# New orders for all five engines behind the prologue of a fused attention and feed-forward kernel

## The chip, the core and the metric

The kernel runs on one core of a Trainium2 chip. The core has a matrix engine (TensorE, in the profile PE, with weight loads as PEld), VectorE (DVE), ScalarE (ACT), GpSimd (POOL) and SyncE (SP). Each engine works through its own list of instructions strictly in order, and engines wait for each other by semaphores. Matrix results land in PSUM, which has eight banks; 16 DMA engines carry data, from queues that SP and POOL fill (ACT issues one store at the end).

The metric is the device time of one launch in microseconds, as the median of a few runs without a profiler.

## The reference

Attention over 4 batches, 8 heads, 768 positions and 64 channels, with a sliding window of 128 positions and 4 sink positions; its output, 3072 tokens of 512 channels, goes through an RMS norm and a gated feed-forward layer (FFN) of width 1536:

```python
scores = scale * np.matmul(q, k.transpose(0, 1, 3, 2))
keep = is_sink | in_window
a = softmax(np.where(keep, scores, -1e9))
x = (a @ v), heads side by side          # 3072 x 512
xn = x / np.sqrt(np.mean(x * x, -1) + 1e-6) * rms_g
g = xn @ w_gate
return (g * sigmoid(g) * (xn @ w_val)) @ w_out
```

Inputs and output are float32.

## The kernel before

The tokens are cut into 24 blocks of 128 (six per batch). Each block goes through the same stages.

- *Loads.* POOL issues DMAs that load q, k and v of a block and change them to bf16 on the way (`load_bf16` L360, `load_v` L364), and the weights `wg`, `wv`, `wo` (L406, L412).
- *Transposes.* q and k are needed with channels on the partitions. Blocks 0 to 5 are transposed on TensorE (`pe_t` L452) and copied out of PSUM by ACT or DVE (`copy_t` L459). From block 6 on, SP issues a DMA transpose (`dma_t` L466).
- *Scores.* TensorE computes them for keys of the block and queries of this block and the next (`scores` L492, `scores_last` L508, `tri_scores` L570). They need k of the block and q of this and the next block. ACT takes exponentials (L519, L543, L579), DVE masks them (L527, L554, L591), from block 16 on POOL does (L533, L604).
- *Attention times v.* `av` (L613 to L628), in two halves per block. DVE divides by the row sums (`normal` L667, L668), ACT takes the sum of squares (`square` L677), POOL a root (`root` L684), DVE scales the block (`spread` L711, tile `xr`). The result is transposed, for blocks 0 to 5 on TensorE (`pe_x` L726, copied at L732), then by a DMA that SP issues (`dma_x` L738), into tile `xnt`.
- *FFN.* Four blocks make a group G, 0 to 5. Gate and value products are made in chunks of one PSUM bank (`mms` L995, tiles `g` and `v`): in group 0 four times 128 columns of weights by one block of tokens (16 matmuls), in groups 1 and 2 two weight chunks by two blocks (8 matmuls), then one chunk by four blocks (4 matmuls). ACT takes a tanh of the gate (L1002, tile `th`), DVE makes the product `p` (L1008), which frees the gate's bank, and `hT` (L1018), which frees the value's bank. `project` (L1028, tile `o`) runs in three quarters of four matmuls per block, ACT evacuates (`evacuate` L1036, tile `osb`, four buffers) and SP stores (L1040).

The order of everything is written out by hand in tables ahead of the function. The function first lists 1093 numbered steps, each with what it needs and gives; a step is one call of a small function on one engine. `ORDER` holds one list of step numbers per engine, `TURNS` says from which engine's list the next step is taken when the program is written down, and `BANKS` says which PSUM bank each step that takes one gets:

```python
for c in "".join(turns.split()):
    e, ops = ids[c]
    o = self.ops[next(ops)]
    assert o["needs"] <= given, o["gives"]
    for s in o["takes"]:
        i = self.held[s] = int(next(banks))
        assert i not in owner, s
        owner[i] = s
    for s in o["drops"]:
        assert owner.pop(self.held[s]) == s
```

So the tables decide what each engine does after what; the waits follow from the data, the banks and the buffers. The step numbers that the prediction speaks of:

| step | engine | what it is |
|---|---|---|
| 245, 300, 387, 422, 542 | PE | scores of blocks 3, 6, 11, 13, 20 |
| 252, 254 | PE | attention times v, block 3, its two halves |
| 261, 263, 280, 282 | PE | transposes of q4, k4, q5, k5 |
| 262, 264, 281, 283 | ACT or DVE | copies of these out of PSUM |
| 250, 251 | DVE | masks of block 3 |
| 253, 255, 256, 257, 258 | DVE, DVE, ACT, POOL, DVE | two normalisations, square, root 3, scaling of block 3 |
| 259, 260, 297 | PE, ACT or DVE | transposes of x3 and their copy; the copy for block 5 |
| 647, 648, 649, 650 | PE, PE, ACT, DVE | group 0, weight chunks 4 to 7, third block of tokens: gate, value `u(0,4,256)`, tanh, product |
| 639, 640 | ACT, DVE | tanh and product of chunks 8 to 11, second block |
| 692, 697 | PE | the first two gate chunks of group 1 |
| 852, 853 | PE | gate and value chunk (3,0) of group 3 |
| 858, 863, 882 | PE | value chunks (3,1) and (3,2), gate chunk (3,6) |
| 58, 59, 64, 65, 61 | POOL | loads of q6, k6, q7, k7, q8 |
| 74, 80, 312, 334, 350 | POOL | loads of k11 and k13; roots 6, 7, 8 |
| 386, 401, 421 | SP | DMA transposes of k11, k12, k13 |
| 681, 756 | SP | stores of group 0, block 1, and group 1, block 0 |

Of the kernel before, what the change touches and what calls it, by code (L numbers as in the profile page):

```python
# [76 lines left out]
692 693 300 698 712 679 323 309 702 307 687-689 331 329 703 707 717 339 317 713 718 355  # L77
# [14 lines left out]
218 227 229 228 230 196 614 221 237 619 240 629 634 644 649 624 262 639 246 248 247 281  # L92
249 283 266-269 256 198 285 287 654 260 659 664 275 669 293 297 675 699 685 694 301 303
304 302 714 324-327 704 311 690 333 680 709 719 340 318 341-343 356-359 349 320 372 755
373-375 734 365 388 724 390 381 749 729 739 744 760 405 403 404 784 406 779 423 424 396
425 426 774 789 799 794 413 432 765 419 439 809 440 441 770 442 455 814 456 824 457 458
448 804 471-474 835 464 829 819 489 491 504-507 524 525 840 526 483 527 497 854 859 869
514 864 850 879 874 894 884 536 520 543-546 899 889 909 845 562 904 563-565 581 555
582-584 934 944 949 574 600 602 959 939 593 964 954 969 915 974 925 920 608 984 979 930
989 1024 1019 1010 1014 1029 1044 1039 1005 1054 1034 1049 1000 1069 1064 1059 995 1085  # L100
1075 1080 1088 1089
# [23 lines left out]
""",  # L125
    "SP": """
# [18 lines left out]
"""  # L145
BANKS = """
0123456701234567012345645645635654353153753470347203563513613256506154632712712475602405
4062430145376241536207134527063456237056514705145415743610547601345716403571263425076134
2510677432510645612036514027635014726145732153570650471621506423710614725634726531027465
4614062576120357230575467145620741546205741632573401567234015321764537465127546246315270  # L150
1215273072504102313672065312675316
# [1009 lines left out]
```

## Time and profile before

| | |
|---|---|
| median of 3 runs | 239.07 us (238.98 to 239.96) |
| the profiled execution's own time | 241.29 us |
| its span, first to last instruction | 239.6 us |
| TensorE busy | 230.0 us (96%) |
| DVE, ACT, POOL busy | 165.8, 118.3, 103.5 us |
| granted TensorE clock | 1.000 |
| DMA, POOL's queue (q0) | 81,760 packets, 84.3% of 16 engines' span |
| DMA, SP's queue (q1) | 35,074 packets, 31.8% |
| load of q, k, v, issue to landing, median | 6.2, 6.9, 6.5 us |
| DMA transpose of q, k, of x | 4.7, 4.8, 2.5 us |

A line of the timeline has start and length in us, engine, source line, operation, what it writes and reads, how many were merged, and in brackets the engine's idle time before it with what ended that. A line of waits has engine and line, whom it waited for, the total in us, how often, and the longest. The chain follows the work that ended last back through what released it. An `SPq` line is SP issuing a DMA. TensorE's matmuls are pipelined: the length of a line is not its cost, the distance to the next start is.

### The profile page before, as it was taken

What the parts mean: (1) busy time and instruction counts of PE and PEld (TensorE: products, weight loads), DVE (VectorE), ACT (ScalarE), POOL (GpSimd) and SP (SyncE); (2) the same over time, 40 slices, a digit from 0 to 9 for tenths busy, and PEclk for the clock granted to TensorE, in tenths of its full rate; (3) what the DMA queues carried; (4) which work ended last, traced back from release to release, by engine and by line L of the source; (5) the groups of instructions that cost most, each with busy time, mean ns of one, the idle gap of its engine ahead of it and who ended that gap; (6) DMA issues with size and microseconds to landing.
All of it is one profiled execution on the core that took longest, in us unless ns stands there. A gap on an engine that the chain in (4) does not pass through costs nothing.

```text
span 239.6 us, 5770 instructions
## 1 busy us (share of the span) xinstructions
PE 230.0 (96%) x2306; PEld 146.5 (61%) x2330; DVE 165.8 (69%) x356; ACT 118.3 (49%) x260; POOL 103.5 (43%) x137
## 2 busy tenths in 40 slices
PE   7988999999999997999999999999999999999994
PEld 5667997967685785866786544454444444444443
DVE  2599888866997898887976689784775246537520
ACT  4676559418686455636574651755531421233112
POOL 7975894059275376219297580438410000000000
PEclk9999999999999999999999999999999999999999
DMA  9999999999999999989999999303500210401024
GB/s 123 147 183 193 185 175 193 155 94 158 162 128 148 158 159 144 130 162 167 132 127 155 180 173 175 79 13 31 81 0 0 47 39 27 172 3 48 0 88 175
DMA packets 117004, 28.20 MB, mean 118 GB/s; under 512 B 107121, under 2 KB 114033, under 8 KB 116978
## 3 DMA queue, kind: packets, MB, share of 16 engines
q0 software_dynamic: 81760, 13.90, 84.3%
q1 hardware_dynamic: 35074, 13.74, 31.8%
q8 instruction: 18, 0.29, 0.5%
q10 hardware_dynamic: 144, 0.20, 0.2%
q14 instruction: 8, 0.07, 0.1%
HBM read 28.35 MB, written 6.29 MB: 145 GB/s over the span
## 4 chain that ended last, share of the span: by engine, by line
PE 84%; DMA 7%; POOL 5%; issue 1%; SPq 1%; ACT 0%; DVE 0%; POOLq 0%; ACTq 0%
PE o L1028 25%; PE g L995 24%; PE v L995 24%; DMA wg<-in_moe_w_gate_dram 4%; DMA qkT<-k 3%; PE s L570 3%; PE av L628 2%; PE av L623 2%; POOL v L364 1%; PE o_last L1048 1%; POOL k L360 1%; POOL wg L406 1%; POOL q L360 1%; PE s L492 1%; POOL wv L406 1%
## 5 line engine op out<-in xcount | busy, mean ns | idle before, releaser
L995 PE MATMUL v<-xnt,wv 128*128 128x128 bf16 (+2 forms) x524 | 71.4, 281 | 0.4 <-DMA wv<-in_moe_w_val_dram 0.2
L995 PE MATMUL g<-xnt,wg 128*128 128x128 bf16 (+2 forms) x525 | 71.1, 282 | 0.6 <-DMA wg<-in_moe_w_gate_dram 0.4
L1002 ACT ACTIVATE th<-g 128x512 bf16<-128x512 f32 x72 | 41.4, 600 | 51.0 <-PE g L995 49.8
L1028 PE MATMUL o<-wo,hT 128*128 128x512 bf16 x259 | 65.4, 379 | 1.1 <-issue 0.2
L1008 DVE SCALAR_TENSOR_TENSOR p<-th,g 128x512 bf16<-128x512 bf16 x72 | 48.2, 681 | 23.2 <-ACT th L1002 22.8
L1018 DVE TENSOR_TENSOR hT<-p,v 128x512 bf16<-128x512 bf16 x72 | 48.2, 685 | 13.7 <-PE v L995 9.8
L995 PEld LDWEIGHTS <-wv 128*128 128x128 bf16 x528 | 43.2, 98 | 19.7 <-DMA wv<-in_moe_w_val_dram 0.6
L995 PEld LDWEIGHTS <-wg 128*128 128x128 bf16 x528 | 42.7, 98 | 20.2 <-issue 0.9
L684 POOL TENSOR_TENSOR rp<-ms,nhalf 128x1 f32<-128x1 f32 x21 | 13.4, 637 | 69.2 <-ACT sq L677 69.2
L1028 PEld LDWEIGHTS <-hT 128*128 128x128 bf16 x276 | 25.9, 98 | 27.7 <-issue 0.2
L579 ACT ACTIVATE e<-s 128x384 bf16<-128x384 f32 x52 | 22.5, 500 | 8.0 <-PE s L570 8.0
L677 ACT ACTIVATE sq<-xall 128x516 bf16<-128x516 bf16 (+1 forms) x24 | 15.2, 634 | 16.6 <-DVE xall L668 16.6
L1036 ACT ACTIVATE osb<-o 128x512 f32<-128x512 f32 x23 | 13.6, 600 | 18.9 <-PE o L1028 15.6
L364 POOL DMA_DIRECT2D v<-in_v_dram x24 | 21.8, 911 | 0.6 <-DMA wv<-in_moe_w_val_dram 0.4
L711 DVE SCALAR_TENSOR_TENSOR xr<-xall,rp,gb 128x512 bf16<-128x512 bf16 x21 | 16.6, 789 | 7.4 <-POOL rp L684 7.4
L668 DVE TENSOR_TENSOR xall<-av,rden 128x256 bf16<-128x256 f32 x48 | 20.4, 424 | 1.7
L360 POOL DMA_DIRECT2D q<-in_q_dram x23 | 20.9, 915 | 0.9 <-POOLq L1142 0.8
L360 POOL DMA_DIRECT2D k<-in_k_dram x23 | 20.8, 909 | 0.9 <-DMA wv<-in_moe_w_val_dram 0.4
L543 ACT ACTIVATE e<-s 128x512 bf16<-128x512 f32 (+1 forms) x36 | 15.3, 516 | 3.6 <-PE s L492 2.5
L604 POOL TENSOR_SCALAR_AFFINE_SELECT e<-e 128x512 bf16<-128x512 bf16 x20 | 13.5, 693 | 6.7 <-ACT e L579 6.5
L628 PE MATMUL av<-v,e 128*128 128x65 bf16 x192 | 16.2, 193 | 0.0
L667 DVE RECIPROCAL rden<-av 128x4 f32<-128x4 f32 x48 | 8.4, 176 | 11.2 <-PE av L628 10.9
(82 smaller groups left out, 180.1 us busy)
## 6 DMA issues: line engine op xcount, KB each, us to landing
out_dram<-osb SPq DMA_DIRECT2D x23, 256.0 KB, 3.6
v<-in_v_dram POOLq DMA_DIRECT2D x24, 128.0 KB, 6.5
q<-in_q_dram POOLq DMA_DIRECT2D x23, 128.0 KB, 6.2
k<-in_k_dram POOLq DMA_DIRECT2D x23, 128.0 KB, 6.9
wo<-in_moe_w_out_dram POOLq DMA_DIRECT2D x2, 768.0 KB, 9.7
wg<-in_moe_w_gate_dram POOLq DMA_DIRECT2D x5, 256.0 KB, 9.1
wv<-in_moe_w_val_dram POOLq DMA_DIRECT2D x5, 256.0 KB, 8.0
qkT<-q SPq DMA_TRANSPOSE x18, 4.7
```

The lines of the kernel that those rows point to most:

```text
L360: nc.gpsimd.dma_start(out=T[name, g], in_=block_of(src, g))
L364: nc.gpsimd.dma_start(out=V16[b][:, t, :, 0:D], in_=block_of(v, g))
L543: nc.scalar.activation(out=e_tile(g)[:, x:x + 2, n0 * P:n1 * P], in_=ps.rearrange("p (j c) -> p j c", c=256)[:, :, n0 * P:n1 * P], func=AC ...
L579: nc.scalar.activation(out=e_tile(g)[:, x:x + 2, 0:TW], in_=BANK.pop(("s", g, u, hi))[:, 0:2 * TW].rearrange("p (j c) -> p j c", c=TW), fu ...
L628: nc.tensor.matmul(out=dest, lhsT=T["e", g][:, x, 0:P], rhs=V16[b][:, t, h, :], start=(t == 0), stop=True, skip_group_check=True,)
L668: nc.vector.tensor_tensor(out=T["x16", g][:, 4 * u:4 * u + 4, :], in0=pvv[:, :, 0:D], in1=rden.unsqueeze(2).to_broadcast((P, 4, D)), op=AL ...
L711: nc.vector.scalar_tensor_tensor(out=T["xr", g], in0=xall[:, g % 3, 0:DM], scalar=r, in1=gb, op0=ALU.mult, op1=ALU.mult,)
L995: nc.tensor.matmul(out=ps[:, i * n:(i + 1) * n], lhsT=w_sb[:, kt, ft * P:(ft + 1) * P], rhs=T["xnt", G][:, kt, cols], start=(kt == 0), sto ...
L1002: nc.scalar.activation(out=T["th", key], in_=BANK[("g", key)], func=ACT.Tanh, scale=0.5,)
L1008: nc.vector.scalar_tensor_tensor(out=T["p1", key], in0=T.pop(("th", key)), scalar=1.0, in1=BANK.pop(("g", key)), op0=ALU.add, op1=ALU.mult,)
L1018: nc.vector.tensor_tensor(out=T[hk][:, i:i + n, cols], in0=T.pop(("p1", key)).rearrange("p (n c) -> p n c", n=n), in1=BANK.pop(("v", key)) ...
L1028: nc.tensor.matmul(out=BANK[("o", G, tb)], lhsT=T["h", G, ft // 4][:, ft % 4, tb * P:(tb + 1) * P], rhs=wo[:, ft, :], start=(ft == 0), sto ...
```

## The change

The tables were made anew, with DMA transposes and stores counted at the times that the last trace shows. The source of the steps is the same, so no instruction is added, removed or changed in shape. All five lists differ from a point behind the prologue on (at about 25 us in the profile of before), and so do `TURNS` and `BANKS`. Four steps change engine: the PSUM copies 260, 281, 283 and 297 go from ACT to DVE. Everything else stays on its engine at another place.

```diff
--- before.py
+++ after.py
@@ -72,83 +72,83 @@
 136 170 150 113 199 124 175 180 168 166 187 137 142 149 201 135 126 130 185 165 122 162
 121 132 203 129 140 222 147 204 209 241 145 163 224 214 191 216 156 138 116 195 114 226
 612 146 148 160 133 151 613 167 161 243 220 233 127 235 159 131 627 117 617 632 628 239
-618 647 642 633 643 622 637 623 261 638 245 648 263 280 652 282 265 197 252 254 653 284
-677 672 271 273 259 682 657 658 662 667 668 289 291 663 278 673 683 684 678 296 674 697
-692 693 300 698 712 679 323 309 702 307 687-689 331 329 703 707 717 339 317 713 718 355
-708 752 345 347 753 371 319 754 757 758 363 361 732 722 733 759 387 379 737 377 747 723
-727 738 728 742 748 743 402 782 392 394 777 778 422 797 772 787 773 783 411 788 762 409
-767 768 430 792 428 763 793 764 769 438 807 798 808 822 454 812 446 802 444 813 832 833
-470 834 462 460 817 827 803 823 818 837 838 503 839 479 481 828 493 847 495 848 523 849
-862 867 510 512 852 853 857 877 842 534 858 843 863 868 532 872 878 892 873 844 882 542
-897 893 883 887 907 902 888 561 551 908 903 553 898 580 932 942 947 917 933 948 572 570
...
+618 642 633 647 643 622 637 623 261 638 245 263 280 652 282 265 254 252 653 197 284 682
+677 259 648 657 662 672 271 273 658 667 668 289 291 663 683 673 678 278 674 296 684 692
+693 697 300 698 712 679 702 323 687 309 307 688 689 703 713 331 329 707 708 717 339 317
+718 752-754 319 355 347 345 757 758 371 722 723 361 363 759 732 737 733 727 747 387 379
+377 728 748 742 738 767 743 768 402 394 782 777 772 392 797 783 422 773 792 409 778 411
+762 787 763 428 788 793 430 798 769 764 438 807 812 808 822 813 454 446 444 802 837 838
+803 832 470 833 462 460 827 817 823 839 828 818 834 479 481 847 848 842 843 503 849 862
+857 852 844 872 495 858 493 863 877 867 523 853 878 873 512 892 510 887 868 902 532 534
+893 882 883 888 542 907 927 903 897 908 928 561 553 898 917 551 918 580 919 929 570 572
...
 """,
     "ACT": """
 25 21 23 200 178 176 179 177 183 181 182 184 169 189 223 205-207 212 208 213 210 192 211
-218 227 229 228 230 196 614 221 237 619 240 629 634 644 649 624 262 639 246 248 247 281
-249 283 266-269 256 198 285 287 654 260 659 664 275 669 293 297 675 699 685 694 301 303
...
-373-375 734 365 388 724 390 381 749 729 739 744 760 405 403 404 784 406 779 423 424 396
...
+218 227 229 228 230 196 614 221 237 619 629 240 644 634 624 262 649 639 248 246 249 247
+266-268 256 198 654 269 285 287 659 664 669 275 293 675 694 685 699 303 301 714 302 304
...
     "DVE": """
 0 2 8 1 3 6 12 11 15 7 173 171 14 13 188 4 186 194 202 190 193 242 225 215 217 316 219
-231 232 234 236 615 238 620 616 630 621 244 635 631 5 636 645 646 625 626 650 640 641
-651 264 250 251 253 255 270 258 288 655 656 286 272 274 660 661 665 277 290 666 292 295
-279 670 700 671 695 696 701 306 315 305 715 310 308 328 705 332 330 313 706 335 710 720
...
+231 232 234 236 615 238 616 620 630 631 645 621 646 635 625 244 636 626 650 264 640 281
+251 250 283 255 253 641 258 260 270 651 655 286 665 656 660 288 274 661 272 418 290 292
+277 295 279 670 297 666 671 695 700 701 696 315 305 306 715 705 310 308 328 706 716 332
...
     "POOL": """
 26 9 10 27-29 32 35 31 33 38 36 30 39 34 40 42 43 41 44 46 48 45 49 47 50 51 54 55 37 53
-52 56 57 59 64 58 65 257 61 276 60 294 66 68 67 62 70 71 73 63 312 74 334 69 72 79 77 83
-76 350 80 82 75 366 382 92 78 97 89 85 91 81 88 84 397 86 414 94 433 100 87 95 107 109
-90 98 449 93 475 103 478 465 477 96 476 490 492 110 99 106 101 484 528 531 529 498 530
...
+52 56 57 257 64 59 58 60 65 61 276 294 73 71 66 68 67 62 63 70 312 79 334 69 76 77 83 74
+82 72 350 80 366 75 382 78 84 85 81 88 91 86 97 397 89 414 433 87 93 90 94 92 95 98 449
+100 465 475 478 476 477 109 99 104 107 96 102 103 105 101 106 484 490 492 110 498 531
...
 """,
     "SP": """
-20 22 24 17 16 19 18 321 299 298 322 337 353 338 369 354 370 385 676 314 336 386 401 681
-420 352 400 368 756 436 421 437 452 384 686 487 468 399 521 691 453 761 469 416 488 501
-502 540 435 522 451 467 559 771 597 598 836 486 766 578 541 579 851 841 560 517 500 539
...
+20 22 24 17 16 19 18 298 299 322 321 337 354 353 338 385 676 369 370 314 336 386 681 420
+401 400 352 368 436 421 437 468 452 487 384 399 761 756 691 453 686 469 416 521 501 435
+488 502 766 451 467 522 771 540 559 846 541 597 578 579 486 851 500 836 560 598 517 539
...
 TURNS = """
 ASDDDDSPGPPDDPPPSPPPPPGPPGPDPGDDPDSGASGASPPPPGDSPPPPPPPDGPADDPGPPAAGAPAAPPPGADPPPPAPDPGAPPPPDAPPDGAPPDPG
-PDAPGPPAPPGAADGPADPAPDGPDAPPAPGDAPPADPAGPADAPPPGPPAAADGPADGPPPPPAPPDPGPPDDPAGPDPAGPDGPDPAGAPDGPDGDAPDGPD
...
+PDAPGPPAPPGAADGPADPAPDGPDAPPAPGDAPPADPAGPADAPPPGPPAAADGPADGPPPPPAPPDPGPPDDPAGPDPAGPDGPDPAGADPGDPAGDPGDPA
...
 BANKS = """
 0123456701234567012345645645635654353153753470347203563513613256506154632712712475602405
-4062430145376241536207134527063456237056514705145415743610547601345716403571263425076134
...
+4062431045213562705340321547231752614715401370140103514720751034217053167420531624075631
...
```

More of the change, by code (lines that the diff above doesn't have):

```diff
@@ L91 @@
 25 21 23 200 178 176 179 177 183 181 182 184 169 189 223 205-207 212 208 213 210 192 211
-218 227 229 228 230 196 614 221 237 619 240 629 634 644 649 624 262 639 246 248 247 281
-249 283 266-269 256 198 285 287 654 260 659 664 275 669 293 297 675 699 685 694 301 303
-304 302 714 324-327 704 311 690 333 680 709 719 340 318 341-343 356-359 349 320 372 755
-373-375 734 365 388 724 390 381 749 729 739 744 760 405 403 404 784 406 779 423 424 396
[L96 to L101, printed above, removed]
+218 227 229 228 230 196 614 221 237 619 629 240 644 634 624 262 649 639 248 246 249 247
+266-268 256 198 654 269 285 287 659 664 669 275 293 675 694 685 699 303 301 714 302 304
+324 704 325 326 680 327 311 690 709 333 719 340-343 318 320 356-358 755 359 349 372 724
+373-375 365 734 729 388 749 739 381 390 760 744 403 404 784 405 779 406 774 396 423-426
+799 794 789 413 432 419 439 809 440 814 441 442 770 765 824 455 804 456-458 448 471-474
+829 464 819 835 840 489 491 506 483 859 507 864 845 850 854 504 505 874 879 497 524-526
+869 527 894 889 884 514 536 543 904 544 909 545 546 899 520 562-565 581-584 920 930 555
+600 934 602 944 939 574 954 949 959 593 969 608 974 989 964 984 925 979 1024 1019 1010
+915 1014 1029 1044 1039 1005 1054 1034 1049 1000 1069 1064 1059 995 1085 1075 1080 1088
+1089
 """,
@@ L119 @@
 26 9 10 27-29 32 35 31 33 38 36 30 39 34 40 42 43 41 44 46 48 45 49 47 50 51 54 55 37 53
[5 rows of a table removed]
[3 rows of a table added]
+528-530 515 537 547 549 548 111 550 566 108 568 567 569 601 588 603 585-587 556 575 594
+609
 """,
     "SP": """
[4 rows of a table removed]
[4 rows of a table added]
 """,
@@ L147 @@
 0123456701234567012345645645635654353153753470347203563513613256506154632712712475602405
-4062430145376241536207134527063456237056514705145415743610547601345716403571263425076134
-2510677432510645612036514027635014726145732153570650471621506423710614725634726531027465
-4614062576120357230575467145620741546205741632573401567234015321764537465127546246315270
-1215273072504102313672065312675316
+4062431045213562705340321547231752614715401370140103514720751034217053167420531624075631
+4017352601675321075207351462705104652170652175204156014525602154637120514367014376041652
+4307074370615207164305714365210745312074531625703162517302517364051260465374021752412562
+0741313204267364131504652134502135
 """
```

16 lines of the change are left out of this document (8 added, 8 removed), and 28 rows, old and new, of the table ORDER.

## The prediction

> **What bounds the kernel now.** I read the busy shares first, then TensorE's waits, then its timeline around the longest one, then the queues that feed that place.
>
> ```profile
> span 239.6 us, 5770 instructions
> ...
> PE 230.0 (96%) x2306; PEld 146.5 (61%) x2330; DVE 165.8 (69%) x356; ACT 118.3 (49%) x260; POOL 103.5 (43%) x137
> ...
> PEclk9999999999999999999999999999999999999999
> ...
> PE 84%; DMA 7%; POOL 5%; issue 1%; SPq 1%; ACT 0%; DVE 0%; POOLq 0%; ACTq 0%
> ```
>
> TensorE is busy 96% of the span at full clock and is 84% of the chain that ended last. The change begins behind the prologue, at about 25 us. From there on a new order can take away only time in which TensorE waits. Its waits:
>
> ```profile
> PE s L570 <- DMA qkT<-k: 1.4, 1, 1.4
> PE warm L428 <- DVE zeros L290: 1.3, 1, 1.3
> PE k L452 <- DMA k<-in_k_dram: 0.6, 1, 0.6
> PE g L995 <- DMA wg<-in_moe_w_gate_dram: 0.4, 1, 0.4
> ```
>
> All but the first lie in the prologue. The first is the scores of block 13 (step 422), late because the DMA transpose of k of block 13 (step 421) took 7.4 us, as the chain shows:
>
> ```profile
> 93.42 1.04 PE L995 MATMUL v<-xnt,wv 128*128 128x256 bf16 x8
> 95.89 0.54 PE L570 MATMUL s<-qkT 64*64 64x192 bf16 x24 [1.42 <-DMA qkT<-k]
> ```
>
> ```profile
> 87.03 1.28 SPq L466
> 88.31 0.04 issue
> 88.36 0.02 SPq L466
> 88.37 0.03 issue
> 88.40 7.44 DMA qkT<-k
> ```
>
> Eight matmuls over 256 columns are 0.87 us from start to start (1.75 us for sixteen in the chain), so step 422 was due at 94.3 and began at 95.9: 1.6 us lost. That is all there is to win.
>
> The second thing to read is how little room the other queues have early on. First ACT, then DVE:
>
> ```profile
> 28.65 1.08 ACT L1002 ACTIVATE th<-g 128x512 bf16<-128x512 f32 x2 [1.31 <-PE g L995]
> 31.33 0.60 ACT L1002 ACTIVATE th<-g 128x512 bf16<-128x512 f32 x1 [1.59 <-PE g L995]
> 33.34 0.58 ACT L459 COPY qkT<-q 128x512 bf16<-128x512 bf16 x1 [1.41 <-PE q L452]
> 33.82 0.60 ACT L1002 ACTIVATE th<-g 128x512 bf16<-128x512 f32 x1
> ```
>
> ```profile
> 33.72 1.42 DVE L1008 SCALAR_TENSOR_TENSOR p<-th,g 128x512 bf16<-128x512 bf16 x2
> ...
> 36.45 0.42 DVE L459 COPY qkT<-k 128x512 bf16<-128x512 bf16 x1
> 36.79 1.28 DVE L554 TENSOR_TENSOR e<-e,masks 128x1024 bf16<-128x1024 bf16 x2
> ```
>
> Rows of one kind give the spacing in a full queue: ACT about 0.49 us (a tanh of 0.60 starts 0.48 behind the copy), DVE 0.6 to 0.7 for a `p`, `hT` or `e` row and 0.34 behind a copy.
>
> **The change, part by part.** No instruction is added or taken away. Every order, the turns and the bank list are new from about 25 us on, and four PSUM copies go from ACT (0.58 us) to DVE (0.42 us). Matmul work is the same, so the sum holds only waits of TensorE.
>
> *The wait at step 422.* Ahead of it the new order puts three chunk halves and two `o` quarters more, and one half less: 3 x 0.87 + 2 x 0.86 - 0.87 = 3.5 us. It is due at 94.3 + 3.5 = 97.8, later still by what the next part adds. On SP the transpose of k13 now stands seven steps behind that of k11 (six transposes at 1.3 and a store at 0.55; store 756 has moved behind it). That one waits for its load until 81.1 (below), so k13's leaves at 81.1 + 1.3 + 7.8 + 0.55 = 90.7 and lands at 95.5 with the median of 4.8, at 98.3 with the trace's longest, 7.6; due 97.8 + 1.1 = 98.9. **-1.6**; what is late next is block 11. Bounds -1.6 and, if the landing slid as far as its due time, 0.
>
> *New waits at 34 to 42 us.* This part has hardly any cover. The gate chunk of step 647 moves back by two chunks, and its tanh (step 649, before at 29.1) now stands behind the copy of q4 (step 262) on ACT. That copy cannot start before 33.34, because TensorE transposes q4 at 32.92 in both orders. So the tanh runs at 33.82 to 34.43, and its DVE product (0.68) at 34.46 to 35.15. The new bank list gives the bank it frees to the transposes of q5 (step 280), which TensorE reaches at 34.13 + 0.33 to 0.54 (scores 3) + 0.22 = 34.7 to 34.9: 0.3 to 0.5 of waiting.
> On DVE there follow k4's copy, a product, q5's copy (moved from ACT) and only then the two masks of block 3: 34.46 + 0.61 + 0.35 + 0.61 + 0.34 = 36.4 for the first, 37.0 to 37.7 for the second. TensorE, from 35.17: 0.22 + 0.89 + 0.32 + 0.48 + 0.36 = 37.45 for the second attention product. It waits 0.25.
> The transposes of x3 (step 259) are due at 41.3, because `u(0,4,256)`, 0.9 us that used to stand early, now follows them. Their input: normalisations done at 39.15, square 0.83, root 0.91, scaling 0.75, ready at 41.7. Another 0.4.
> Together **+1.1**, between 0.8 (shortest of each) and 1.3. A gain here is excluded: the old order waits nowhere in this stretch. The other three moved copies are hidden: that of k5 ends on DVE at 38.0 and its scores are due at 39.3.
>
> *Loads and transposes of blocks 6 and 7.* Root 3 now stands ahead of the loads of q7, k6 and q6 on POOL. They leave at 40.9 instead of 33.4 to 36, with v6, k7 and q8 behind them. q6 leaves at 42.6 and with the page's median of 6.2 lands at 48.8; SP then issues q6, k6, k7, q7 at 1.3 each, so q7 leaves at 52.7 and lands at 57.5 with the median of 4.7. Scores 6, at 57.2 before with the same work ahead, are due at 58.3. Cost 0; with the longest transpose of the trace (7.6) it is 2.0.
>
> *Block 11.* On POOL the load of k11 moves from behind root 6 to behind root 7 and four loads. Root 7 was at 67.19; attention 7 has two chunk halves more ahead (1.75), and the 1.1 comes on top: 70.0. Plus 0.56 and 4 x 0.9, k11 leaves at 74.2. At the page's k median of 6.9 it lands at 81.1; its transpose, which holds SP until then, lands at 85.9 at the median of 4.8. Scores 11, at 81.64 before, have four halves more ahead: due at 81.64 + 3.5 + 1.1 = 86.2. On time by 0.3 at the medians; with a load of 8.0 (the longest of k's DMAs between 60 and 80) and a transpose of 7.6 it is 3.6 late. Bounds 0 and +3.6. I take **+0.5**, near the medians, because fewer transposes run beside these loads than in the old order.
> The Trainium skill, page "DMA: Bandwidth & Descriptors", section "Anatomy of one DMA — SWDGE (gpsimd) path", puts such a transfer at about 2.0 us plus its bytes over 436 GB/s: for 128 KB an estimate of 2.3 us. By it k11 would land at 76.5, this term would be 0 and the sum 0.5 lower; the trace's medians of 6.2 to 6.9 disagree, and I go by them.
>
> *Late waits of a few tenths.* Step 853 now takes the bank that product (3,0) frees. Between the end of step 863 and 853 TensorE has 2.0 us, and DVE must fit `hT`, a normalisation and that product: 0.60 + 0.56 + 0.68 and two hand-overs. Step 542 has 1.5 us behind gate chunk (3,6) for a tanh, a product and what stands before it. Each comes out at 0 to 0.3, and the old order's own small wait before step 858 (0.2) goes. **+0.2**, between -0.2 and +0.6.
>
> *The rest.* Attention 17 to 19 come about 10 us later on TensorE, with that much more FFN work ahead of them, so the loads and POOL masks of those blocks, which trade places, have more time: 0. Stores are off TensorE's path unless `osb` buffers run out; those of group 0 move back by about 6 us at 101 to 107, with evacuation (1,2) due some 5 us behind. Cost 0, bounds 0 and 1.
>
> **Sum**: -1.6 + 1.1 + 0 + 0.5 + 0.2 = +0.2 us on the profiled execution. That one took 241.29 us, 239.6 of it span and 1.7 around it; the median of the runs is 239.07, 2.2 lower. Carried over to the median: 239.3.
>
> **Rivals.**
> *A, the sum as worked out*: 239.3, own range 238.2 to 240.2.
> *B, block 11 (slower).* One mechanism: k11's late load and its transpose with everything behind it on SP. For it: individual DMAs beside full queues take 7 to 8 us. Against: the SP queue is quiet while it waits. It decides from a landing 1.5 us past due, 87.7. With 2.0 to 3.6 in place of 0.5: 240.8 to 242.4, middle 241.3.
> *C, the wait at step 422 is not in unprofiled runs.* For it: the median lies 2.2 us under the profiled execution, more than the wait itself. Against: transposes beside loads are slow at many places, which no recording explains. The 1.6 is then not won: 240.9.
> *D, the early waits do not come.* Then -1.6 + 0.2, with block 11 in time: 237.7; with its 0.5, 238.2. Against it, the ACT order is strict in every row. It needs the tanh of step 649 before 33.3.
> *E, block 11 is in time with room*: 238.8. For it: transposes of `xnt`, many of them beside fewer loads, have a median of 2.5 us. The formula of the Trainium skill's DMA page would have it so.
>
> **How the numbers follow.** A 0.44, B 0.22, C 0.12, D 0.12, E 0.07, unnamed waits of 1.5 us and more in all 0.03. About 0.5% (1.2 us) is what this measurement can tell from no change. Faster is D but for its upper end: 0.10. Slower is B, C and the unnamed: 0.37. The rest, A, E and 0.02 of D: 0.53. The range 238.0 to 241.6 leaves out most of D and the upper part of B.
>
> **What would show it.** In the profile after: no wait on `qkT<-k` before the scores of block 13; TensorE gaps of 0.2 to 0.5 us between 34 and 42, with the tanh behind the q copy on ACT at 33.8; group 1's first gate chunk at 55.6 instead of 54.5; k11's load leaving at about 74 and scores 11 at 86 or later. I am wrong if the tanh runs at 30, if scores 11 wait over 1.5 us, or if a queue that I cost at nothing, blocks 6 to 8 or the `osb` buffers, holds TensorE.

## The result and the profile after

The changed kernel takes 240.51 us (median of 6 runs, 240.23 to 240.9); the kernel before, timed beside it, 239.3 us. The ratio is 1.0049 with a 95% interval of 1.0033 to 1.0066: half a per cent slower, on the border of what counts here as no change, and certainly not faster. A second measurement on another chip gave 1.0045 [1.0029, 1.0062]. The forecast was 239.3 us in a range of 238.0 to 241.6: the time lies in the range, 1.2 us above the value named. It was made on a median of 239.07, so it stood for +0.2 us, and +1.2 us was measured.

Times of one kernel differ from chip to chip (medians of before from 239.3 to 240.6 us), and single executions can be some us longer than the rest; the longest (20 in all, over 1.5% above the shortest, 17 of them with a granted clock of 0.991 to 0.993) are left out of the ratios, and each ratio is taken against the kernel before on the same chip.

The profiled execution of after took 240.9 us. Its page, the lines that answer to those shown of before:

```profile
span 239.2 us, 5761 instructions
...
PE 230.7 (96%) x2303; PEld 147.0 (61%) x2330; DVE 166.8 (70%) x360; ACT 116.0 (48%) x256; POOL 103.7 (43%) x137
...
PEclk9999999999999999999999999999999999999999
...
PE 80%; POOL 6%; issue 5%; DVE 4%; DMA 3%; ACT 1%; POOLq 0%; DVEq 0%; ACTq 0%
```

TensorE is as busy as before and at full clock. So the question is once more what it waits for. Its six longest waits in the profile of after (engine and line, whom it waited for, total, times, longest, in us):

```profile
PE warm L428 <- DVE zeros L290: 1.3, 1, 1.3
PE av L628 <- POOL e L533: 0.7, 1, 0.7
PE k L452 <- DMA k<-in_k_dram: 0.2, 1, 0.2
PE s L474 <- DVE bias L305: 0.2, 1, 0.2
PE warm L428 <- DVE qkT L459: 0.2, 1, 0.2
PE g L995 <- ACT esk L769: 0.2, 1, 0.2
```

The wait of 1.4 us for the transposed keys of block 13 is gone, as forecast. The timeline shows the scores (L570) following their predecessor without a gap:

```profile
96.74 1.04 PE L995 MATMUL v<-xnt,wv 128*128 128x256 bf16 x8
97.71 0.54 PE L570 MATMUL s<-qkT 64*64 64x192 bf16 x24
```

In its place stands a wait that the prediction had put at nothing: the second half of attention 17 (L628) for masks that POOL makes (L533).

```profile
138.37 0.19 PE L623 MATMUL av<-v,e 128*128 128x65 bf16 x1
139.27 0.20 PE L628 MATMUL av<-v,e 128*128 128x65 bf16 x1 [0.70 <-POOL e L533]
```

The POOL part of the same timeline shows why:

```profile
131.23 1.78 POOL L364 DMA_DIRECT2D v<-in_v_dram x2
132.97 0.93 POOL L360 DMA_DIRECT2D q<-in_q_dram  x1
133.83 0.93 POOL L364 DMA_DIRECT2D v<-in_v_dram  x1
134.70 0.94 POOL L360 DMA_DIRECT2D k<-in_k_dram  x1
136.10 0.88 POOL L360 DMA_DIRECT2D q<-in_q_dram  x1 [0.46 <-DMA v<-in_v_dram]
136.99 0.58 POOL L684 TENSOR_TENSOR rp<-ms,nhalf 128x1 f32<-128x1 f32 x1
137.53 1.69 POOL L533 TENSOR_SCALAR_AFFINE_SELECT e<-e 128x512 bf16<-128x512 bf16 x2
```

POOL issues ten loads in a row from 127.7 us on, each some 0.9 us long. Ahead of the last it stands still for 0.46 us until an earlier load (v of block 19) has landed. The two masks of block 17 stand behind all of that, end at 139.2, and TensorE, which began attention 17 at 138.2, goes on at 139.27. From start to start of its steps it loses 0.88 us. About half of that is the 0.46 us; the other half is the second mask, which took 1.09 us here and 0.62 to 0.71 in the other profiles with the new late order.

One more thing must be read before the two executions are subtracted. Before's profiled execution was 2.2 us above its median, after's only 0.4. A long execution of before is being set beside a common one of after.

### The profile page after: what moved, and what is told of

Read it like the earlier page. It is cut to its first block, busy times and chain, and to the rows that moved or that the text cites. A ratio compares the mean times of both kernels' runs of the same rounds, so it can differ in the third digit from the quotient of the medians.

```text
span 239.2 us, 5761 instructions
## 1 busy us (share of the span) xinstructions
PE 230.7 (96%) x2303; PEld 147.0 (61%) x2330; DVE 166.8 (70%) x360; ACT 116.0 (48%) x256; POOL 103.7 (43%) x137
## 4 chain that ended last, share of the span: by engine, by line
PE 80%; POOL 6%; issue 5%; DVE 4%; DMA 3%; ACT 1%; POOLq 0%; DVEq 0%; ACTq 0%
PE v L995 24%; PE g L995 22%; PE o L1028 20%; DMA v<-in_v_dram 3%; PE av L628 2%; PE s L570 2%; PE av L623 2%; POOL q L360 1%; PE warm L428 1%; PE o_last L1048 1%; POOL k L360 1%; POOL rp L684 1%; POOL v L364 1%; PE s L492 1%; PE s L474 1%
## 5 line engine op out<-in xcount | busy, mean ns | idle before, releaser
L995 PE MATMUL v<-xnt,wv 128*128 128x128 bf16 (+2 forms) x527 | 73.0, 282 | 0.2
L1002 ACT ACTIVATE th<-g 128x512 bf16<-128x512 f32 x72 | 41.7, 600 | 57.6 <-PE g L995 51.9
L1036 ACT ACTIVATE osb<-o 128x512 f32<-128x512 f32 x23 | 13.1, 602 | 25.0 <-PE o L1028 25.0
L711 DVE SCALAR_TENSOR_TENSOR xr<-xall,rp,gb 128x512 bf16<-128x512 bf16 x21 | 16.0, 766 | 4.2 <-POOL rp L684 4.1
L628 PE MATMUL av<-v,e 128*128 128x65 bf16 x192 | 16.1, 193 | 0.8 <-POOL e L533 0.7
L628 PEld LDWEIGHTS <-e 128*128 128x128 bf16 x192 | 12.7, 98 | 3.2 <-POOL e L533 0.8
```

The costliest lines, as they stand in the source:

```text
L628: nc.tensor.matmul(out=dest, lhsT=T["e", g][:, x, 0:P], rhs=V16[b][:, t, h, :], start=(t == 0), stop=True, skip_group_check=True,)
L711: nc.vector.scalar_tensor_tensor(out=T["xr", g], in0=xall[:, g % 3, 0:DM], scalar=r, in1=gb, op0=ALU.mult, op1=ALU.mult,)
L995: nc.tensor.matmul(out=ps[:, i * n:(i + 1) * n], lhsT=w_sb[:, kt, ft * P:(ft + 1) * P], rhs=T["xnt", G][:, kt, cols], start=(kt == 0), sto ...
L1002: nc.scalar.activation(out=T["th", key], in_=BANK[("g", key)], func=ACT.Tanh, scale=0.5,)
```

## The experiments

All variants change only the tables: the order lists, with turns and banks to match. Every time in this part that is read from a trace is from that kernel's own profiled execution.

### Was the 1.6 us really there? The kernel before a second time

No edit.

> The kernel before, unchanged, profiled a second time. Theory 1 (the profile of before stands for its runs): scores 13 wait for the transposed keys of block 13 again, by 1.2 to 1.8 us, and the profiled execution is again about 2 us over the median. Theory 2 (the profiled execution of before was a late one, and the wait is shorter in the runs that are timed): the wait is under 0.8 us, and the profiled execution lies within 0.7 us of the median. The time itself: ratio 1.000 to before by both.

239.59 us median of 12 runs, ratio 0.9978 [0.9955, 1.0001]; the profiled execution took 239.29, 0.3 under that median. The ratio compares a kernel with itself: the 35 runs of before on this chip have a median of 240.17 and reach from 238.90 to 244.66. So a difference of half a us between medians can be nothing on this chip, and the rows of the traces have to carry the smaller terms. TensorE's waits in it:

```profile
PE warm L428 <- DVE zeros L290: 1.3, 1, 1.3
PE k L452 <- DMA k<-in_k_dram: 0.6, 1, 0.6
PE s L474 <- DVE bias L305: 0.2, 1, 0.2
PE v L995 <- DMA wv<-in_moe_w_val_dram: 0.2, 1, 0.2
PE o L1028 <- issue: 0.2, 1, 0.2
```

No line for the keys of block 13 at L570. The timeline at that place:

```profile
92.77 1.04 PE L995 MATMUL v<-xnt,wv 128*128 128x256 bf16 x8
93.84 0.54 PE L570 MATMUL s<-qkT 64*64 64x192 bf16 x24
```

Eight matmuls, 0.87 us together, from 92.77 on make the scores due at 93.64; they begin 0.2 us later, not 1.6. Even 0.1 of that is no wait: where the keys lie ready, these scores begin 0.97 us behind the start of such a chunk (96.74 to 97.71 in the profile of after). So the wait was 1.5 us in the first profile and is 0.1 us here. In the trace of this execution the transpose of k13 was issued at 87.25 and landed at 93.80, 6.55 us; in the first profile 88.40 and 95.84, 7.44 us. Counted from a fixed step of the prologue's end (step 638, at 33.14 and 32.48), SP issued it 0.5 us earlier and the DMA was 0.9 us shorter. Theory 2: the first profile showed an execution with a late transpose. What the change could win here in a common execution is 0.1 us.

### The same question from TensorE's side

```diff
-727 738 728 742 748 743 402 782 392 394 777 778 422 797 772 787 773 783 411 788 762 409
+727 738 728 742 748 743 402 782 392 394 777 778 797 422 772 787 773 783 411 788 762 409
```

> The kernel before with one exchange on PE: the gate half of group 2, chunk 10 (step 797) goes ahead of scores 13 (step 422), so the scores are asked for one half of 0.87 us later, and nothing else moves. Theory 1 (the wait of 1.42 us at scores 13 is in the timed runs too): the half runs in the wait, 0.9 us less, 238.4 us, less what the exps of block 13 lose behind it. Theory 2 (the timed runs wait there for 0.5 us at most): 0 to 0.5 us less, 238.8 to 239.3 us.

240.01 us median, ratio 1.0006 [0.9977, 1.0034]; no gain. In its profiled execution the scores waited for nothing, and the next gate chunk waited instead, for the exponentials of block 13 that now start later:

```profile
94.45 0.54 PE L570 MATMUL s<-qkT 64*64 64x192 bf16 x24
95.41 1.80 PE L995 MATMUL g<-xnt,wg 128*128 128x256 bf16 x15 [0.42 <-ACT e L579]
```

A cover of 0.87 us for a wait that is mostly not there buys nothing and costs a new wait. This agrees with theory 2 in that nothing is won; the times that it named (238.8 to 239.3) were too low.

### The keys of block 13 earlier

```diff
-420 352 400 368 756 436 421 437 452 384 686 487 468 399 521 691 453 761 469 416 488 501
+420 352 400 368 421 756 436 437 452 384 686 487 468 399 521 691 453 761 469 416 488 501
```

> The kernel before with one step moved on SP: the DMA transpose of block 13's keys (421) goes ahead of a store (756) and of block 14's query transpose (436), so it is issued 2.5 us earlier. Theory 1 (in some executions these keys land after scores 13 are due, as in the first profile of before, and that is where its runs of 240 us and more come from; in the second profile they landed 0.04 us ahead): no wait at the scores of block 13, the median 0 to 0.3 us below before, and the spread of the runs much narrower than that of before on the same chip, nothing above 241 us. Theory 2 (before's longer runs come from elsewhere): median and spread as before's.

239.9 us median, 239.89 for before on the same chip; ratio 0.9994 [0.9963, 1.0025]. The profiled execution took 239.23 and has no wait at these scores: the keys landed at 88.4, and the scores begin at 93.84, 0.96 us behind the chunk ahead of them. The common execution gains nothing that can be measured, for the third time. On the spread: its 12 runs lie between 238.83 and 241.16, one above 241; of 29 runs of before on that chip, 238.87 to 244.09, six lie above 241. (For the three longest of these the granted clock was 0.991 to 0.993, for the others 0.999 or more, so late keys are not the only candidate.) That fits theory 1, but with one in five of before's runs that long, twelve runs with one or none come about by chance one time in four. It is not settled.

### The changed kernel a second time

No edit.

> The changed kernel, unchanged, profiled a second time. Theory 1 (its early loss of 0.66 us, its waits of 0.6 us at 112 to 117 us, and the wait of attention 17 for POOL's masks belong to the order): all three again, the last within 0.2 us of 0.88. Theory 2 (the wait of attention 17 hangs on one load that landed late, v19, and POOL idles 0.46 us for it by chance): the first two again, the last under 0.5 us.

240.41 us median, ratio 1.0045 [1.0029, 1.0062], profiled execution 240.7. The waits of the same kind that the first profile of after shows at 110 to 115 us came again to the hundredth: 0.34 us ahead of gate chunk step 812 for a bank that ACT's sink exponentials free, and 0.24 us in attention 14 for its masks. The first of them, in the first profile of after (a chunk of eight matmuls is 0.87 us from start to start):

```profile
109.41 1.05 PE L995 MATMUL g<-xnt,wg 128*128 128x256 bf16 x8
110.62 1.03 PE L995 MATMUL g<-xnt,wg 128*128 128x256 bf16 x8 [0.16 <-ACT esk L769]
```

The early stretch, from step 638 to the first gate chunk of group 1, took 21.84 us (22.00 in the first profile, 21.33 in both of before). But attention 17 did not wait at all; another step did, scores 6 (step 300):

```profile
56.06 1.04 PE L995 MATMUL g<-xnt,wg 128*128 128x256 bf16 x8
57.62 0.61 PE L492 MATMUL s<-qkT 64*128 64x256 bf16 x8 [0.52 <-PE g L995]
```

They begin 1.56 us behind the start of the chunk, 0.97 in the first profile: 0.59 us lost. (Counted from a due time at 56.93, without the 0.1 us that such a change takes anyway, it is 0.69.) The releaser that the line names is not it; by the DMA completions in the trace the transposes of block 7's queries, which scores 6 read as well, landed at 57.53. They are the last of four in the new order of SP, and SP issued them slowly (51.94 to 54.00, 2.1 us in place of the usual 1.2). In the first profile of after they landed 2.0 us ahead of the scores.

So there are two kinds of loss in after. Some stand in both profiles: 0.5 to 0.7 us early, 0.6 us at 110 to 115. Some come in one execution and not in the next: 0.88 us at attention 17, 0.59 us at scores 6. Theory 2 holds.

### POOL's loads behind the masks of block 17

```diff
-100 465 475 478 476 477 109 99 104 107 96 102 103 105 101 106 484 490 492 110 498 531
+100 465 475 478 476 477 109 99 104 107 96 102 103 490 492 105 484 101 106 110 498 531
```

> The changed kernel with four of POOL's loads (v21, k20, q22, root 16; steps 105, 484, 101, 106) put behind the two masks of block 17 (490, 492). Theory 1 (POOL issuing ten loads back to back holds the masks up, and attention 17's second half waits for them, as the trace of after shows with 0.7 us at av and some 0.9 us by the row sum): 0.7 to 0.9 us less than after, 239.6 to 239.8 us, and no wait of av for e of POOL. Theory 2 (PE would then wait at the next step for something else that is late, the keys or values of block 20 and 21 now loaded some 1.5 us later): within 0.3 us of after, with the wait at another line.

Three of the ten loads and a root now stand behind the masks. 240.41 us median, ratio 1.0005 [0.9976, 1.0033]; profiled execution 240.33. The wait is gone, nothing followed it, and the masks now end at 135.4:

```profile
134.08 1.29 POOL L533 TENSOR_SCALAR_AFFINE_SELECT e<-e 128x512 bf16<-128x512 bf16 x2
135.26 0.94 POOL L364 DMA_DIRECT2D v<-in_v_dram  x1
```

From step 638 to the end it took 202.98 us, against 203.77 in the first profile of after: 0.79 less, as theory 1 has it for an execution that has the wait. This is the chip on which before spread so widely, so the ratio tells little. Beside the 12 runs of the unchanged kernel there (239.59 us) this version is 0.8 us longer, and by the rows, from step 638 to the end, 1.0 us longer than the second profile of before (202.98 against 201.98). So the masks of block 17 are not the steady loss.

### Which stretch of the order costs it: four splices

The early order of before (up to the first gate chunk of group 1, 54 us), the rest of after; of the edit, TensorE's first lines:

```diff
-618 642 633 647 643 622 637 623 261 638 245 263 280 652 282 265 254 252 653 197 284 682
-677 259 648 657 662 672 271 273 658 667 668 289 291 663 683 673 678 278 674 296 684 692
+618 647 642 633 643 622 637 623 261 638 245 648 263 280 652 282 265 197 252 254 653 284
+677 672 271 273 259 682 657 658 662 667 668 289 291 663 278 673 683 684 678 296 674 692
...
```

> The orders of before up to the first gate chunk of group 1 (some 54 us), the orders of after from there. Theory 1 (the new early order costs what the row sum shows between 33 and 54 us, 0.67 us): 0.6 to 0.7 us less than after, 239.8 us. Theory 2 (that loss is given back where the next wait ends, since loads run by the clock and not by PE's progress): within 0.2 us of after, 240.3 to 240.6 us.

239.69 us median, ratio 0.9985 [0.9955, 1.0014], on the chip where the unchanged kernel before gave 239.59 in 12 runs. With the early order put back the changed kernel loses nothing that the runs can tell (0.14 us by the rows from step 638 to the end, 202.13 against 201.98). That is 0.7 us less than the version with the POOL masks mended, which kept the new early order, on the same chip, and 0.86 us less by the rows: theory 1. Its profiled execution took 239.3 us; attention 17 did not wait there: POOL's masks end at 137.49, and TensorE comes to the matmuls that read them at 137.56. POOL was not held up in its row of loads this time.

The other way round, the new early order with the rest of before:

```diff
-618 647 642 633 643 622 637 623 261 638 245 648 263 280 652 282 265 197 252 254 653 284
-677 672 271 273 259 682 657 658 662 667 668 289 291 663 278 673 683 684 678 296 674 697
+618 642 633 647 643 622 637 623 261 638 245 263 280 652 282 265 254 252 653 197 284 682
+677 259 648 657 662 672 271 273 658 667 668 289 291 663 683 673 678 278 674 296 684 697
...
```

> The orders of after up to the first gate chunk of group 1 (some 54 us), the orders of before from there. Theory 1 (what the early order costs stays until the end): 0.6 to 0.7 us more than before. Theory 2 (PE coming 0.66 us later meets the keys of block 13 with room, and gets 0.1 to 0.3 us of the loss back there): 0.3 to 0.5 us more than before.

242.28 us median of all eight runs, 241.25 of the five that the ratio takes; ratio 1.0082 [1.005, 1.0113]. The profiled execution, 239.95 us, was its shortest, and is 0.66 us longer than the second one of before. That this is the number of theory 1 is chance: 0.31 us of it lie in the prologue, which the edit leaves alone (step 638 at 32.79 against 32.48). From step 638 to the end it takes 202.35 us against 201.98, 0.36 more: the early stretch 21.84 against 21.33, and 0.14 got back behind it, 0.1 of that at the keys of block 13. That is what theory 2 says. But six of the eight runs were above 241, and no trace shows what they waited for. The sign is clear, the size in the timed runs is not explained.

The last stretch alone (before's order up to 115 us, after's from there):

```diff
-767 768 430 792 428 763 793 764 769 438 807 798 808 822 454 812 446 802 444 813 832 833
+767 768 430 792 428 763 793 764 769 438 807 798 808 822 454 812 446 802 444 813 837 838
...
```

> The orders of before up to the first output chunk of group 2 (step 832, some 115 us), the orders of after from there. Theory 1 (the masks of block 17 behind ten loads cost 0.5 to 0.9 us wherever PE stands): 0.5 to 0.9 us more than before, with a wait of av for e of POOL. Theory 2 (they are late only by chance of a load): within 0.3 us of before, and no such wait over 0.2 us.

239.77 us median, ratio 1.0016 [0.9991, 1.0041], profiled execution 239.48, attention 17 without a wait: theory 2. But in this splice eight loads stand ahead of the masks, not ten, and they end at 136.07, 1.5 us before TensorE begins attention 17. That ten loads need not cost anything either, the profile of the first splice shows, with some 0.1 us of room.

And the middle alone, 54 to 115 us:

```diff
-677 672 271 273 259 682 657 658 662 667 668 289 291 663 278 673 683 684 678 296 674 697
-692 693 300 698 712 679 323 309 702 307 687-689 331 329 703 707 717 339 317 713 718 355
+677 672 271 273 259 682 657 658 662 667 668 289 291 663 278 673 683 684 678 296 674 692
+693 697 300 698 712 679 702 323 687 309 307 688 689 703 713 331 329 707 708 717 339 317
...
```

> The orders of after from the first gate chunk of group 1 to the first output chunk of group 2 (some 54 to 115 us), those of before ahead of it and behind it. Theory 1 (this stretch takes away the risk at scores 13 and costs 0.3 to 0.6 us in small waits at 112 to 117 us): 0 to 0.4 us more than the shortest runs of before, with no run above 241 us. Theory 2 (the middle is where the change loses): 0.8 us or more over before.

240.09 us median, ratio 1.0026 [0.999, 1.0061], four of twelve runs above 241, so theory 1 missed. The profiled execution was a long one (243.15 us) and shows its waits:

```profile
PE s L508 <- DMA qkT<-k: 1.2, 1, 1.2
PE s L492 <- DMA qkT<-k: 1.1, 1, 1.1
PE g L995 <- ACT e L579: 0.8, 1, 0.8
```

They are transposed keys again, of blocks 17 and 18, at 127 to 129 us. The chain of that execution leads back to the load of k17, issued at 113.8 us; the second profile of before has it at 85.3. The order of after loads k17 as late (114.2 in its first profile), but comes to the scores of block 17 only at 132.2 us. Here the order of before takes over at 115 us and asks for them at 126.1. So it is the seam of this splice that makes the load late, and this run says nothing clean on the middle; it shows once more what a late key transpose does to this kernel.

### What in the early stretch: two exchanges

```diff
-218 227 229 228 230 196 614 221 237 619 629 240 644 634 624 262 649 639 248 246 249 247
+218 227 229 228 230 196 614 221 237 619 629 240 644 634 624 649 262 639 248 246 249 247
...
-20 22 24 17 16 19 18 298 299 322 321 337 354 353 338 385 676 369 370 314 336 386 681 420
+20 22 24 17 16 19 18 298 299 321 322 337 354 353 338 385 676 369 370 314 336 386 681 420
```

> The changed kernel with two exchanges in its early order: on ACT the tanh of step 649 goes ahead of the copy of block 4's transposed queries (262), and on SP the transposes of block 7's queries (321) go ahead of those of its keys (322). Theory 1 (the early loss is the bank that this tanh gives up late, 0.30 us of 0.66 us, and, in some executions, the queries of block 7 that land after scores 6 are due, 0.69 us in the second profile of after): no wait at the transposes of block 5's queries, none at scores 6, the drift up to 54 us down from 0.66 to 0.36 us, and the ratio to before down from 1.0045 to 1.001 to 1.003. Theory 2 (the next wait takes over: block 4's scores behind the later copy, or attention 3 behind the exponentials): drift as before, 0.6 us and more, ratio 1.004 and more.

240.58 us median beside 240.61 for before on a chip where before spread widely (239.46 to 245.12): ratio 1.0005 [0.9976, 1.0033], which tells little. The trace tells more. First before, where a value chunk (648) stands between scores 3 and the transposes of block 4's keys and block 5's queries (`PE L452 k` and `q`):

```profile
34.67 1.07 PE L995 MATMUL v<-xnt,wv 128*128 128x128 bf16 x16
35.58 0.39 PE L452 MATMUL k<-ident,k 128*128 128x128 bf16 x4
35.80 0.39 PE L452 MATMUL q<-ident,q 128*128 128x128 bf16 x4
36.02 1.06 PE L995 MATMUL g<-xnt,wg 128*128 128x128 bf16 x16
```

Then after, where the tanh of step 649 stands behind the copy and the transposes of block 5's queries (`PE L452 q`) come 0.53 us behind those of block 4's keys:

```profile
32.99 1.09 ACT L1002 ACTIVATE th<-g 128x512 bf16<-128x512 f32 x2
33.63 0.69 DVE L1008 SCALAR_TENSOR_TENSOR p<-th,g 128x512 bf16<-128x512 bf16 x1 [0.28 <-ACT th L1002]
33.84 0.40 PE L452 MATMUL k<-ident,k 128*128 128x128 bf16 x4
33.96 2.09 ACT L543 ACTIVATE e<-s 128x512 bf16<-128x512 f32 x4
34.37 0.38 PE L452 MATMUL q<-ident,q 128*128 128x128 bf16 x4
34.62 1.05 PE L995 MATMUL g<-xnt,wg 128*128 128x128 bf16 x16
```

And the version with the exchange:

```profile
34.01 0.40 PE L452 MATMUL k<-ident,k 128*128 128x128 bf16 x4
34.11 2.06 ACT L543 ACTIVATE e<-s 128x512 bf16<-128x512 f32 x4 [0.35 <-PE s L492]
34.24 0.39 PE L452 MATMUL q<-ident,q 128*128 128x128 bf16 x4
34.76 1.05 PE L995 MATMUL g<-xnt,wg 128*128 128x128 bf16 x16
```

The transposes now follow at 0.23 us, without a wait. The next step, gate chunk 652, then waits 0.29 us: the bank list gives it the bank of one half of scores 3, which the first of the four exponentials (34.11 to some 34.7) frees. The stretch up to group 1's first gate chunk takes 21.98 us, as in after. For the drift theory 2 holds. In after both waits end at nearly the same time, so only the first shows. Behind both stands one move: value chunk 648 ran between scores 3 and the transposes before, 0.9 us in which the exponentials could begin, and now runs elsewhere. In this execution scores 6 (57.17) did not wait: with block 7's queries first, these landed at 52.1 and the keys at 54.7. A single profile can't show that this will hold. It has neither of the two occasional waits, and takes 202.96 us from step 638 to the end, 1.0 more than the second profile of before.

### Two attempts at a version that beats both

The first: the early order of before with the rest of after (as above), and three mendings.

```diff
-396 423-426 799 794 789 413 432 419 439 809 440 814 441 442 770 765 824 455 804 456-458
+396 423-426 799 794 789 413 419 432 439 809 440 814 441 442 770 765 824 455 804 456-458
...
-800 412 790 795 791 431 796 801 429 415 434 810 815 811 443 816 825 805 445 447 806 459
+800 412 790 795 791 431 796 801 429 415 434 810 815 443 811 816 825 805 445 447 806 459
...
-100 465 475 478 476 477 109 99 104 107 96 102 103 105 101 106 484 490 492 110 498 531
+100 465 475 478 476 477 109 99 104 107 96 102 103 490 492 105 484 101 106 110 498 531
```

> The early order of before, the later one of after, and three mendings in it: POOL's four loads behind the masks of block 17; ACT's sink exponentials of group 2 (step 419) ahead of the mean square of block 13 (432); DVE's masks of block 14 (443) ahead of a gate product (811). Theory 1 (each wait that the trace of after shows is worth its length): 0.4 us less than the early order of before with the rest of after had (239.3 us in its profiled execution, 4.9 us by the sum of PE's delays), and 0.2 to 0.3 us less than before. Theory 2 (other waits take their places): within 0.2 us of before.

240.45 us median, ratio 1.0046 [1.0029, 1.0063]: other waits took their places, as in theory 2, and it is slower than either theory had it. The scores of block 15 wait for a bank that the moved product frees:

```profile
PE s L570 <- DVE hT L1018: 1.0, 1, 1.0
```

Moving a mask forward, to save 0.24 us, pushed a product `hT` (step 811) back whose bank TensorE needed sooner. The second attempt leaves DVE's list alone:

```diff
-396 423-426 799 794 789 413 432 419 439 809 440 814 441 442 770 765 824 455 804 456-458
+396 423-426 799 794 789 413 419 432 439 809 440 814 441 442 770 765 824 455 804 456-458
...
-100 465 475 478 476 477 109 99 104 107 96 102 103 105 101 106 484 490 492 110 498 531
+100 465 475 478 476 477 109 99 104 107 96 102 103 490 492 105 484 101 106 110 498 531
```

> The early order of before and the later one of after, with POOL's four loads behind the masks of block 17 and the sink exponentials of group 2 (419) ahead of the mean square of block 13 (432); DVE's order is left as it is in after, so the scores of block 15 have no bank to wait for. Theory 1: 0.2 us less than the early order of before with the rest of after had in its profile, 239.1 us there, and the runs within 0.3 us of before's shortest, none above 241 us. Theory 2 (a wait comes up elsewhere): 239.5 us and more.

240.21 us median, ratio 1.0002 [0.9976, 1.0027], 12 runs between 239.51 and 240.98. The bank of the sink exponentials is waited for no longer, but this execution (240.75 us) lost 1.4 us to two loads that landed late, of `wo` and of a v:

```profile
PE o L1028 <- DMA wo<-in_moe_w_out_dram: 0.8, 1, 0.8
...
PE av L628 <- DMA v<-in_v_dram: 0.6, 1, 0.6
```

No version beats the kernel before by an amount that these runs can tell.

## Why the prediction was right and where it was wrong

The value 239.3 was 1.2 us too low, 0.2 of that for the median it was built on. Rival C, with 0.12, came nearest: its 240.9 stands beside 240.51. I had put the sum (A) first. C's condition held, but that its number is so near is partly luck: of its +1.8 us the 0.5 of block 11 never came, and the 1.1 of the early stretch was 0.5 to 0.7; waits that no rival named made up for some of it.

**The wait at step 422, -1.6: the mechanism held, the size failed.** The new order does take the wait away, with over 3 us to spare in both profiles of after. But the 1.6 us (1.5 without the 0.1 that the change to the scores takes anyway) belonged to the one execution that was profiled. A second profile shows 0.1 us, and covering the wait, in two ways, gained nothing. The warning stood in the text: the profiled execution lay 2.2 us above the median of the runs. I carried the sum over to the median as if the whole difference were a constant. Of all the steps this is the one that failed by most.

**New waits at 34 to 42 us, +1.1: right in kind, measured 0.5 to 0.7.** Beginning from step 638 the stretch up to group 1's first gate chunk takes 22.00 and 21.84 us against 21.33. (By the clock of the trace that chunk began at 54.3 us, not at the 55.6 named: the prologue, which the change leaves alone, ended 0.83 us earlier in this execution, and the rest is the smaller loss.) The tanh stood behind the q copy as forecast: it began at 32.99, which is 33.82 with the 0.83 put back. The transposes of q5 waited 0.30 (I had 0.3 to 0.5), attention 3 lost 0.13 + 0.12 (0.25). In the first profile another 0.2 us went ahead of an output product at 39.0, in the second not. The 0.4 at the transposes of x3 did not come: the root that feeds it took 0.56 us, not 0.91. The tanh was about half the cause; with it out of the way the exponentials of block 3 hold the next step as long. The splices bear out that this stretch is the main part of what makes after slower: without it 0.9985 [0.9955, 1.0014], with it alone 1.0082 [1.005, 1.0113].

**Blocks 6 and 7, 0:** right in the first profile, 0.59 us in the second, where the queries of block 7 left SP at 51.9 and landed at 57.5. I had 52.7, 57.5 and scores due at 58.3; with the prologue of that execution, 0.66 us earlier, these are 52.0, 56.8 and 57.6. The transpose took 5.6 us from issue to landing where I had 4.7, and TensorE was there at 57.0, because the stretch ahead cost 0.5 and not my 1.1. That a queue which I had at nothing, for blocks 6 to 8, would hold TensorE was one of my signs of being wrong; in this execution it did.

**Block 11, +0.5: measured 0.** Its load left at 73.2 and landed at 78.6, its transpose at 82.1, for scores at about 85. The load took 5.4 us, not 6.9, and the transpose 3.5, not 4.8. Rival B falls, E holds in its outcome. The Trainium skill's formula ("DMA: Bandwidth & Descriptors", section "Anatomy of one DMA — SWDGE (gpsimd) path"), an estimate of 2.3 us for this load, named the right outcome from a figure that the trace does not bear out: 5.4 us.

**Late waits, +0.2: the wrong places.** Steps 853 and 542 waited for nothing measurable. Instead 0.34 us at step 812 and 0.24 in attention 14, in both profiles of after, less the old 0.2 before step 858: +0.4. (With the early order of before the wait at step 812 is about 0.2, so half of it hangs on the early stretch.)

**The rest, 0: failed.** I wrote that the loads and POOL masks of blocks 17 to 19 "have more time". The masks had ten loads put ahead of them, 9 us of POOL's time, and I had not added them up. In one of two profiles that cost 0.88 us, together with a slow mask; with three of the loads behind the masks, the profiled execution is 0.79 us shorter.

Put together from the second profile of before and counted from step 638 to the end (201.98 us), after's two executions come out as -0.1 + 0.67 + 0.34 + 0.24 - 0.2 + 0.88 = +1.8, measured +1.8 (203.77), and -0.1 + 0.51 + 0.59 + 0.34 + 0.24 - 0.2 = +1.4, measured +1.4 (203.39). Without the two occasional waits the terms make 0.8 to 0.95 us. Two profiles that have the new early order and neither of these waits (the POOL masks mended, and the two exchanges) are 1.0 us longer than before's, and the medians of after lie 1.2 and 1.0 above before. So the steady part is most of the loss. How often each occasional wait comes can't be said from two traces. What the long runs of before and of the splice with the new early order wait for stays open too.

## What to carry to other kernels

A wait on a DMA in one profiled execution can be a draw and not a constant: if that execution lies above the median by more than the wait itself, take a second profile before you count the wait as a gain. Where an engine has little cover, list for the next steps all that must be done before each may start; taking away the wait that shows can uncover one of the same length right behind it. And when queues that issue loads are put into a new order, add up the issue time that now stands ahead of each computation on that queue. Compare profiles from a fixed step behind the part that no edit touches: here the prologues alone differed by up to 0.9 us.

## What the runs showed of the hardware

A DMA of the same size at the same place of the same program takes a different time from execution to execution: the transpose of k13 7.44 and 6.55 us in two executions of before. That of q7 landed 2.0 us ahead of its use in one execution of after and held its use up by 0.59 us in another.

SP usually takes 1.2 us to issue a transpose; now and then it took 2.1 to 2.4 (in the second profile of before the longest for keys was 2.41 us), which moves all that follows on that queue.

POOL's tenth load in a row was held for 0.46 us until the load issued eight places earlier had landed. In the trace both signal the same semaphore, one of eight that POOL's loads use in turn, and the later one waits for it. So the hold comes from the waits that the program holds; that POOL itself could not have issued a ninth open load is not shown. In the second profile of after the same load found the earlier one landed (135.91 for a start at 136.20) and was not held.
